# Modulation columns in two passes, Q and K weights in three loads, and a new order of work in an adaLN block (sliding-window attention, then a gMLP mixer)

## The chip, the cores and the metric

One core of one Trainium2 chip runs the kernel. The metric is the device time of one execution in microseconds (us); lower is better. TensorE is called PE, VectorE DVE, ScalarE ACT, GpSimd POOL and SyncE SP, as in the profile.

## The reference, cut to what matters

```python
mod = (silu(c) @ w_mod).reshape(1, 6, 1, 448)      # c: (1, 448), w_mod: (448, 6*448)
sa, ca, ga, sb, cb, gb = mod[:, 0..5]
h = layernorm(x) * (1 + ca) + sa                   # x: (1, 2048, 448), bf16
q, k, v = split(h @ wqkv)                          # 16 heads of 28, wqkv: (448, 3*448)
p = softmax(where(0 <= i - j < 256, q k^T * 28**-0.5, -1e9))
x = x + ga * ((p v) @ wo)
h = layernorm(x) * (1 + cb) + sb
z = gelu(h @ w_in)                                 # w_in: (448, 1792), tanh form
z1, z2 = z[..., :896], layernorm(z[..., 896:])
g = w_sp @ z2 + b_sp                               # w_sp: (2048, 2048), over the sequence
x = x + gb * ((z1 * g) @ w_out)                    # w_out: (896, 448)
```

## The kernel before, in words

The sequence of 2048 rows is cut into 16 tiles of 128 rows, and the tiles into six blocks of 1, 1, 2, 4, 4 and 4 tiles (`blocks` in `PARAMS`). Each engine runs one fixed list of instructions. A small planner holds all operations (`Op`) with their dependencies; a hand-stored list, `ORDER` (L164 to L224), names them by number in the order in which they are put into the engines' lists. Behind a slash stand the choices of buffer (a bank of PSUM, a slot of SBUF), and behind a point the choice of engine where an operation may run on more than one. `Planner.schedule` reads the list, and `Planner.emit` turns every dependency, and every reuse of a buffer, into a semaphore wait. An engine works its own list strictly in order, so a waiting instruction holds all that stand behind it.

**The start.** The row `c` is loaded by ACT's queue (L473), copied in two pieces to a padded row `crz` (`cz0`, `cz1`, L519 and L520; the padding is zeroed by `zc`, L518), turned into columns by four tiny matmuls (`c_cols`) and passed through SiLU into `sc_sb` (L522). Between them PE has 30 matmuls on zeros (`warm0` to `warm29`, L1068 to L1071; the first 12 are 512 wide, the others 256), whose result nobody reads. `mod_cols` (L526 to L540) makes the columns of `sa` and `ca`: eight sums of four matmuls each, `modA0_0` to `modA1_3`, 32 matmuls with a moving operand one column wide; DVE then adds 0 or 1 and writes `modT` (`modAe`, L539). All eight wait for both halves of the modulation weights, `wmodA0` on SP's queue and `wmodA1` on ACT's (`load_dup`, L463 to L467).

The 448 input features do not divide into four chunks of 128, so chunk 1 and chunk 2 overlap: the chunks start at features 0, 128, 192 and 320. `load_dup` loads the overlapping 64 rows twice, in two transfers of 256 rows. `load_ov` (L455 to L461) leaves the doubled rows out: three transfers, one of chunks 0 and 1, one of chunk 3, and one of the upper half of chunk 2.

Each x tile is normalised: statistics on DVE (`l1_*st0`, `ag`, `ve`, L557 to L564), the power -1/2 on POOL (`l1_*rs`, L565), and the scaled tile `xn` on DVE, ACT or POOL (L578, L579, L608). Blocks 0 to 2 are transposed by PE against an identity (`tr`), and the result is multiplied by 1 + `ca` and shifted by `sa` when it is moved from PSUM to `hT` (L641 on ACT, L646 on DVE). Blocks 3 to 5 are transposed by DMA from SP's queue (L663) and modulated in place (`hm`, L655). The raw Q and K weights `wqk_raw` come by two `load_dup` transfers and are copied into the padded form `WQK` by eight copies, `wqkf0_0` to `wqkf1_3` (L679 on DVE, L680 on ACT): one for each chunk 0 to 3 of each half of the heads.

**Attention.** `project` (L719 on) makes Q and K (`qk`, four matmuls for each group of four heads) and V (`v`), moved from PSUM by `qke` (L740 on ACT, L743 on DVE) and `ve` (L751, L754). `S{j}_{u}` are the scores of query tile j, `E{j}_{u}` their exponentials on ACT (L841), `M` the mask on POOL (L847), `PV` the product with V, then come transposes and normalisation (`oq`, `rec`, `nrm`, `oT`), the product with `wo`, and the residual `x1`. One `S` fills PSUM banks for two `E`, and the next `S` in these banks waits for the `E`. `PT` holds the exponentials in 11 slots, which are handed from an `E` to the `PV` that reads it and on to a later `E`.

**The mixer.** After a second normalisation (`l2`, `x2`, `h2T` by DMA, `h2m`), `z2m` and `z1m` are the two halves of `h @ w_in` (`w_in_sb`). Their GELUs run on ACT (`z2g` L945 and L949, `z1g` L968). For five tiles `z2m` is made early and parked raw (`z2e`, L939 on DVE, L942 on ACT). `G` is the product with `w_sp`, whose transposed tiles are read by DMA over SP's queue (L1008) into space freed by attention; `ga`, `gu` (L1037, L1039), `out` and `fin` (L1059) finish the rows, and SP's queue stores them (L1061). Exp and GELU need different function tables on ACT; the switch is an instruction of its own, `ACT_TABLE_LOAD`.

Of the kernel before, what the change touches and what calls it, by code (L numbers as in the profile page):

```python
# [168 lines left out]
148/2 149 155 156 150 151 177/3 176.1/3 178 157.1 486/1 233 98/7 28 99 100 152 101 487 179 123/0 124 125 126 127.1 234 93/1 94 95 96 102.1 97.1 27
103/2 6 104 105 106 107.1 235 238 236 241 18 322 88/0 89 90 91 92 242 243 244/4 138/0 19 139 140 141 245.1/1 142 485/0,0 320 399 108/2 109 110 111  # L170
489/2 158/1 159 160 112 181/3 161 162 180 182 482/2 15 501/1,0 505/4 401 246.1/3 402 198/1 17 199 163/0 164 200 201 165 247.1/2 166 403 202.1 203/3
204 205 206 193/1 194 195 196 502/7 508/1,0 207 218/3 219 167 483 220 188/0 221 248 222.1 189 190 191 192.1 249 197 183/1 184 185 186 213/2 214 187.1
215 216 217.1 509/3 208/3 209 506 511/8 318 210 488/0 323 503 490 491 492/0 493 494.1/1 522/0,1 523/9 211 212.1 526/1 251 228/1 319 223/2 224 225 229
250 230 231 232 316 317 226 227 252 507/0 253 254 321 324 512 510 504 255 529/1,0 530/3 276/3 405 513/0 266/1 267 268 261/2 262 325 326 327/2 331
330.1/3 269 533/10 527 270 277 329/0 263 264 524 536/1,0 539/5 537/0 334 278 279 280.1 271/0 272 311/1 265.1 273 312 514 313 314 274 275.1 550/1,0
296/3 328.1/1 315 297 298 299 300.1 515.1/0 404 406 256/1 257 291/0 258 259 400 407 551/4 552 557/1,2 292 293 294 554/6 260.1 286/1 287 288 289 561/8
564/2,0 516/2 295.1 538/0 558/2 534 540 535 525 528 495/1 408 409 531 532 555 562 332 559 290.1 281/1 282 567/7 578/0,1 283 284 541/0 517/0 518 542
543.1/0 565/3 285.1 579/1 519 520 585/0,2 333 335.1 336.1 544/0 496/1 497 498 499 582/0 917 521 560/0 563 566 568 553 556 337 500 589/10 586/5 569/0
570 592/2,1 593/3 914 545/1 546 547 548 916 412.1/3 369/0 370 371 338.1 583 947 349/3 350 945 549 372 373.1 595/8 606/0,1 607/6 351 610/9 352 364/1
587 365 366 367 353.1 946 613/0,2 915 588/0 614/7 571.1/0 572/1 590 591 596 580 581 584 368.1 594 354/1 355 356 620/0,1 597/0 573/0 574 575 410.1/1  # L180
416 948 949 615 576 617/4 344/2 931/3 577 345 346 347 621/1 623/10 608 357 611 358 413.1/0 960 348.1 962 932 598 950 933 920 634/1,0 934 935 936 414
937 938 618 635/0 306/1 307 411/2 308 309 939 641/1,2 599.1/0 301/0 302 1426 303 304 417 310.1 384/1 638/8 385 386 387 961 600/0 922 645/5 648/0,2 963
964 965 305.1 616/0 619 609 388.1 612 646 622 624 339/1 340 642/3 651/2 662/1,2 639 341 342 636 625/0 637/0 652 649/6 650 643 644 647 640 626 627.1/1
415 418.1 420.1 663/1 669/0,1 343.1 359/1 360 361 362 653/0 374/0 375 376 377 666/7 667 664 673/5 676/1,2 654 670/9 671 679/4 363.1 601/1 602 603
628/2 378.1 629/0 677/3 630 631 951 952.1/1 923 632 633 690/2,0 691/0 421.1 966 604 694/2 605 389/0 390 391 392 697/1,2 394/1 395 396 419.1 967/0
698/10 393.1 442/0 397 919 701/8 398.1 674 443 444 445 704/1,0 655.1/0 379/1 380 446.1 672/0 675 702 975 1428 381 382 953 954/1 955 656/0 383.1 707/6
718/2,0 705/5 665 722/1 699 723 680 678 719/4 668 681/0 657/1 658 682 683.1/0 720 659 660 661 990 991 725/1,0 726/3 727 729/7 730 437/0 438 439 440
452/1 441.1 959.1 976 453 454 455 732/1,2 724/0 721 456.1 728 432/1 433 434 435 977 978 436.1 735/9 746/0,2 684/0 918 969/1 731 733/1 968 695 692 736
# [12 lines left out]
1146 1150 1017.1 888 891 1148 1177 1149 1019 1147 1151 1179 1324 1314/3 1313 1311 1038 1325 1347/0 1348 1180/0 1152/2 1312 1316 1326/5 1315 1181 1349
1335/4 1338/6 1339 1337 1182 898 1331/7 1350 1351 1332 1341 1330 1328 1352 1039 1183 1184 880/0 1040 1433 1129/1 1154 1018.1 899/0 1153 902 1030 892
904 895 896 889 1028 1031 1033 1034 1032 1427 881/2 1451 1131 882 1041 1042/1 1329 905/0 1044/2 1122/1 1123 1106/3 1132/3 1185 1124 1327 906 907.1/1
1371/2 1373 1336 1107 1334 883 1333 884 885 1108 1340 1186 1343 1155 1156 1372 1133 1342 1130 1125 1126 1043 1157 1376/5 1375 1201/1 1202 1374 1045
908/2 1135 1377 1379 1207 1378 1134 1137.1 909/2 910 1204 1203 911 912 1050 1205 1187/0 1380/2 1127 1109 1447 1158 1110 1051 1381 1206 1188 913 1383/0
1385 1384 1074/0 1136.1 1111 1112 1128 1193 1386 1191 1208/2 1215/1 1217 1052 1219 1382 1387 1048.1 1189 1192 1190 1046 1220 1053 1054 1218 1442
1353/3 1049.1 1437 1358/2 1357 1355 1055 1076 1056 1075 1450 1059.1/1 1299/1 1057.1/2 1077 1078 1060 1194/3 1047 1243/0 1248 1245 1058 1356 1209 1210
1211 1212 1079 1354 1216 1388 1080 1249 1359 1361 1196 1305/0 1221 1222/1 1244 1300 1362/2 1457 1213 1214 1448 1364 1441 1360 1195 1197 1247 1246
1250/2 1229/1 1302 1443 1234 1301 1233 1232 1456 1231 1304 1444 1224 1303 1159/0 1163 1160 1435 1306 1223 1252 1165 1062 1064.1 1063 1368/3 1225 1446
1235 1090/0 1162 1061.1 1407/1 1161 1230 1226 1227 1363 1453 1409 1307 1410/0 1412 1164 1366 1365 1408 1251 1253 1198 1228 1236/1 1271/1 1274 1275  # L210
# [73 lines left out]
def bass_adaLN_cond__sliding_block__mixer_gmlp__prompt_kernel(  # L284
# [13 lines left out]
    S, D, H, DH = 2048, 448, 16, 28  # L298
# [139 lines left out]
    def mm(e, out_, lhsT, rhs, st, sp, **kw):  # L438
        return e.matmul(out_, lhsT=lhsT, rhs=rhs, start=st, stop=sp, **kw)  # L439
# [688 lines left out]
```

## Time and profile before

| | us |
|---|---|
| median of 3 runs | 272.41 (272.1 to 272.92) |
| the profiled execution | 271.65 |
| its span, first to last instruction | 269.9 |
| PE busy | 260.3 (96%) |
| DVE busy | 171.8 (64%) |
| ACT busy | 132.0 (49%) |
| POOL busy | 101.2 (37%) |

Busy time counts pipelined matmuls with their modelled ends, so 96% of PE is not 96% of its best rate. The shares are averages over a start of some 17 us, an attention stretch to about 111 us, and a mixer stretch to the end, in which different engines are full.

### The profile page before, as it was taken

Reading aid. Unit: us, or ns where it says so; the run is one execution under the profiler, and the core shown is the slowest. Engines: PE = TensorE matmul, PEld = TensorE weight load, DVE = VectorE, ACT = ScalarE, POOL = GpSimd, SP = SyncE. Lnnn points to the kernel's source line nnn. Section 1 sums busy time; section 2 is a strip of 40 time slices with the busy share of each in tenths; the row PEclk is TensorE's granted clock in tenths of the full one; section 3 lists DMA queues with packets and bytes.
Section 4 is the critical chain, followed back from the end, with each engine's and each line's share of the span. In section 5 each row is a group of like instructions: output and inputs, shape, how many; then the busy total and the mean of one; then the engine's idle time right before and its main releaser. Section 6 shows DMA issues by size and latency. Waiting matters only on the chain.

```text
span 269.9 us, 6339 instructions
## 1 busy us (share of the span) xinstructions
PE 260.3 (96%) x2660; PEld 126.4 (47%) x2689; DVE 171.8 (64%) x413; ACT 132.0 (49%) x177; POOL 101.2 (37%) x160
## 2 busy tenths in 40 slices
PE   7989999999999999999999999999999999999995
PEld 2756445554544454344444444444444444444553
DVE  5789989778889998798986723115242132265444
ACT  5688999999999998986675300000000001000000
POOL 3174789798879996575322300000000000000000
PEclk9999999999999999999999999999999999999999
DMA  7955163691679421637599991000000000000214
GB/s 222 343 188 72 22 163 89 82 163 22 75 122 305 74 52 26 111 73 123 116 220 181 184 192 31 2 0 0 0 2 0 0 0 2 17 0 0 69 53 137
DMA packets 60811, 23.85 MB, mean 88 GB/s; under 512 B 49839, under 2 KB 60654, under 8 KB 60782
## 3 DMA queue, kind: packets, MB, share of 16 engines
q1 hardware_dynamic: 60507, 22.98, 40.9%
q10 hardware_dynamic: 274, 0.46, 0.6%
q8 instruction: 21, 0.34, 0.5%
q14 instruction: 9, 0.07, 0.1%
HBM read 9.53 MB, written 1.84 MB: 42 GB/s over the span
## 4 chain that ended last, share of the span: by engine, by line
PE 79%; DVE 9%; ACT 5%; POOL 3%; issue 2%; DVEq 0%; POOLq 0%
PE ps L439 79%; ACT PT L841 5%; DVE w_out_sb L897 1%; DVE QKT L743 1%; POOL PT L847 1%; POOL hT L655 1%; DVE hT L655 1%; DVE st_all L557 1%; DVE wo_sb L788 1%; DVE oq L873 1%; POOL xn L578 1%; DVE WQK L679 1%; DVE ve_all L564 1%; DVE xn L578 0%; DVE Vaug L754 0%
## 5 line engine op out<-in xcount | busy, mean ns | idle before, releaser
L841 ACT ACTIVATE PT<-ps 128x1024 bf16<-128x1024 f32 x90 | 84.9, 1034 | 3.9 <-PE ps L439 3.5
L1037 DVE TENSOR_TENSOR tmpg<-ps,bsp_bc 128x512 bf16<-128x512 f32 x28 | 18.8, 687 | 58.8 <-PE ps L439 58.6
L968 ACT ACTIVATE z1T<-ps 128x512 bf16<-128x512 f32 x28 | 15.4, 600 | 79.6 <-PE ps L439 79.6
L439 PE MATMUL ps<-QKT,z 128*128 128x512 bf16 x223 | 51.2, 379 | 0.1
L847 POOL TENSOR_SCALAR_AFFINE_SELECT PT<-PT 128x512 f32<-128x512 f32 x60 | 37.5, 647 | 4.0 <-ACT PT L841 3.9
L565 POOL TENSOR_TENSOR rs_all<-ve_all,neghalf 128x1 f32<-128x1 f32 (+2 forms) x30 | 19.9, 666 | 39.1 <-DVE ve_all L564 39.0
L439 PEld LDWEIGHTS ps<-QKT,z 128*128 128x128 bf16 x224 | 21.8, 98 | 26.4 <-ACT z1T L968 0.3
L439 PE MATMUL ps<-hT,WQK 128*128 128x512 bf16 (+2 forms) x179 | 30.9, 304 | 3.0 <-issue 0.8
L439 PE MATMUL ps<-w_in_sb,hT 128*128 128x448 bf16 (+1 forms) x128 | 29.2, 354 | 0.1
L439 PE MATMUL ps<-hT,w_in_sb 128*128 128x512 bf16 (+1 forms) x105 | 27.1, 380 | 0.4 <-DVE hT L655 0.2
L439 PE MATMUL ps<-w_spD,z 128*128 128x512 bf16 x110 | 26.4, 379 | 0.2
L439 PE MATMUL ps<-w_spC,z 128*128 128x512 bf16 x106 | 25.8, 379 | 0.3
L439 PE MATMUL ps<-w_out_sb,z1T 128*128 128x448 bf16 (+2 forms) x119 | 21.5, 342 | 0.0
L557 DVE BATCH_NORM_STATS2 st_all<-z2raw 128x6 f32<-128x448 bf16 x32 | 18.8, 610 | 3.7 <-ACT z2raw L949 2.3
L439 PEld LDWEIGHTS ps<-hT,WQK 128*128 128x128 bf16 x192 | 14.4, 97 | 13.1 <-DVE QKT L743 1.2
L557 DVE BATCH_NORM_STATS2 st_all<-x_sb 128x6 f32<-128x448 bf16 x32 | 19.4, 614 | 1.5 <-DMA x_sb<-in_A_x_dram 1.4
L743 DVE CAST QKT<-ps 128x512 bf16<-128x512 f32 (+2 forms) x34 | 18.5, 558 | 2.6 <-PE ps L439 2.5
L439 PE MATMUL ps<-QKT 28*128 28x128 bf16 x720 | 18.3, 217 | 0.8 <-ACT QKT L740 0.5
L1059 DVE TENSOR_TENSOR fin<-ps,x_sb 128x448 bf16<-128x448 f32 (+2 forms) x17 | 9.8, 595 | 13.6 <-PE ps L439 10.5
L439 PEld LDWEIGHTS ps<-QKT 28*128 28x128 bf16 x720 | 10.4, 92 | 15.3 <-ACT PT L841 10.3
L439 PEld LDWEIGHTS ps<-w_in_sb,hT 128*128 128x128 bf16 (+1 forms) x128 | 10.2, 96 | 15.5 <-issue 5.9
L439 PEld LDWEIGHTS ps<-w_spC,z 128*128 128x128 bf16 x112 | 11.0, 98 | 13.2
(75 smaller groups left out, 304.5 us busy)
## 6 DMA issues: line engine op xcount, KB each, us to landing
wmod_sb<-in_w_mod_dram SPq DMA_DIRECT2D x8, 224.0 KB, 4.6
w_in_sb<-in_B_w_in_dram SPq DMA_DIRECT2D x8, 224.0 KB, 3.2
out_dram<-fin SPq DMA_DIRECT2D x16, 112.0 KB, 1.8
x_sb<-in_A_x_dram SPq DMA_DIRECT2D x3, 448.0 KB, 7.6
wqk_raw<-in_A_wqkv_dram SPq DMA_DIRECT2D x2, 452.0 KB, 6.0
bsp_bc<-in_B_b_sp_dram SPq DMA_DIRECT2D x1, 512.0 KB, 4.2
wmod_sb<-in_w_mod_dram ACTq DMA_DIRECT2D x1, 448.0 KB, 4.1
wmod_sb<-in_w_mod_dram SPq DMA_DIRECT2D x1, 448.0 KB, 4.9
```

Source lines behind the costliest of these rows:

```text
L439: return e.matmul(out_, lhsT=lhsT, rhs=rhs, start=st, stop=sp, **kw)
L557: st = [dve("%sst%d" % (name, i), prio, dve_ns(D), lambda e, i=i, s_=s_: e.bn_stats(st_all[:, slot, t, i, :], s_()), deps, tens) for i, s_ ...
L564: v = dve(name + "ve", prio, 75, lambda e: e.tensor_scalar(ve_all[:, slot, t0:t1], mv_all[:, slot, t0:t1, 1], EPS, None, ALU.add), deps)
L565: r = pool(name + "rs", prio, 420 + 148 * n, lambda e: e.tensor_tensor(rs_all[:, slot, t0:t1], ve_all[:, slot, t0:t1], neghalf[:, t0:t1], ...
L578: return e.tensor_scalar(dst, src, rs_all[:, slot, t:t + 1], nm_all[:, slot, t:t + 1], ALU.mult, ALU.add)
L655: return e.tensor_scalar(hT[:, c_, cols], hT[:, c_, cols], modT[:, base_col + 4 + c_:base_col + 5 + c_], modT[:, base_col + c_:base_col + ...
L743: return e.tensor_copy(QKT[:, g, cols], ps[:, ten.slot, 0:w])
L841: e_op = P.op("E%d_%d" % (j, ui), pr, [("act", 925, lambda e, e_in=e_in, e_out=e_out: e.activation(e_out(), e_in(), ACT.Exp, scale=SCALE)) ...
L847: ready = pool("M%d_%d" % (j, ui), pr - 50, pool_ns(512), lambda e, pt=pt, pat=pat, cm=cm, cmp=cmp: e.affine_select(out=pt32(pt.slot), in_ ...
L968: g = P.op("z1g%d_%d" % (tb, ft), pr - 19, [("act", act_ns(512), lambda e: e.activation(z1T[:, ft, tb * 512:(tb + 1) * 512], ps[:, ten.slo ...
L1037: a = dve("ga%d_%d" % (tb, ft), pr, dve_ns(512), lambda e, tb=tb, ten=ten, tg=tg: e.tensor_tensor(tmpg[:, tg.slot, :], ps[:, ten.slot, :], ...
L1059: fs.append(dve("fin%s%d" % (nm, t), pr, dve_ns(c1 - c0), lambda e, t=t, ten=ten, ft_=ft_, c0=c0, c1=c1: e.tensor_tensor(fin[:, ft_.slot, ...
```

## The change

It does four things.

- `modA` is no longer made by `mod_cols`. There are 16 operations of two matmuls: first chunks 2 and 3 of all eight columns, each waiting only for `wmodA1`, then chunks 0 and 1, waiting for `wmodA0`. The number of matmuls is the same, 32. `mod_cols` is still used for `modB`.
- `wqk` is loaded by `load_ov` (three transfers without the doubled rows) in place of `load_dup` (two).
- A copy `wqkf{g}_{c}` waits only for the transfer that holds its chunk, and a `qk` matmul only for the copy of its chunk; before, both waited for all.
- `ORDER` is new from end to end: positions, engines and buffers of all operations.

```diff
-    t_wqk = load_dup("wqk", -95.5, wqk_raw, A_wqkv, 0, 904, order=t_wmA)
+    t_wqk = load_ov("wqk", -95.5, wqk_raw, A_wqkv, 0, 904)
+    for o in t_wqk:
+        o.order += t_wmA
...
-    t_modA, m1 = mod_cols("modA", -50, (0, 1), 0, t_wmA, CH, 128)
+    mA_ten = Ten(B_D, guard=True)
+    m1 = []
+    for h in (1, 0):
+        for col in range(8):
+            def fn(e, h=h, i=col // 4, mc=col % 4, col=col):
+                last = None
+                for kc in (2 * h, 2 * h + 1):
+                    last = mm(e, ps[:, mA_ten.slot, col:col + 1], wmod_sb[:, kc, i * D + CH[mc]:i * D + CH[mc] + 128], sc_sb[:, kc:kc + 1],
+                              h == 1 and col == 0 and kc == 2, h == 0 and kc == 1, skip_group_check=True)
+                return last
+            m1.append(pe("modA%d_%d%s" % (col // 4, col % 4, "h" if h else ""), -50, 52, fn, [t_wmA[h], t_sc], [mA_ten], order=m1[-1:]))
+    t_modA = [dve("modAe", -49.9, 80, lambda e: e.tensor_tensor(modT[:, 0:8], ps[:, mA_ten.slot, 0:8], zero_one[:, :], ALU.add), m1 + t_zo, [mA_ten])]
...
-                ("pool", 620, lambda e, d=dst, s_=src: e.tensor_copy(d, s_))][0:2 if r0 else 3], t_wqk, port=True))
+                ("pool", 620, lambda e, d=dst, s_=src: e.tensor_copy(d, s_))][0:2 if r0 else 3], [t_wqk[(0, 0, 2, 1)[c_]]], port=True))
...
-                    e, ps[:, ten.slot, 0:n_], stat(k), mov(k), k == 0, k == 3), [deps, hT_op[b][k]], [ten], order=ops[-1:]))
+                    e, ps[:, ten.slot, 0:n_], stat(k), mov(k), k == 0, k == 3), [deps[k] if isinstance(deps, dict) else deps, hT_op[b][k]], [ten], order=ops[-1:]))
...
-                ops, ten = chain("qk%d_%d" % (b, g), p_, t_wqkp[u // 2] + [z_qk],
+                ops, ten = chain("qk%d_%d" % (b, g), p_, {k: [t_wqkp[u // 2][k]] + ([z_qk] if k == 2 else []) for k in range(4)},
```

What the new list makes of the engines' orders, where it differs most:

- PE: before, `warm0, warm1, c_cols, warm2 to warm11, modA0_0, warm12 to warm14, modA0_1 to modA1_3`, then transposes and the other warm matmuls. After: `warm0 to warm15`, the four `tr0`, `warm16, warm17, c_cols, warm18 to warm20, tr1_0_0`, the 16 parts of `modA`, `warm21 to warm27`, and on.
- DVE: `cz0`, `cz1` and `zc` stand behind the statistics of tile 0 and tile 1; before, they stood ahead of them. Four of the eight `wqkf` are on DVE (before: six), one on ACT (two), three on POOL (none).
- ACT: `xn1` stands ahead of the SiLU. Up to the second exponential there are, after `modT`: four `hT` moves, one `wqkf`, nine `qke`, `E0_0`, four `qke`. Between the second exponential and the last `S`, ACT has 3 `ve` (before 5), 4 `qke` of 256 columns (2), 3 of 512 (2), none of 128 (1), and 2 `z2e` (4); the move of the second half of `hT2` is there in both.
- ACT at the end of attention: before, `E15_4, E15_5`, one table load, the GELUs. After: `E15_4`, table load, `z1g0_5, z1g0_4`, table load, `E15_5`, table load, the other GELUs. `E15_5` takes over the `PT` slot of `E14_1`, and so waits for `PV14_1`.
- PE at the end of attention: the six `PV14` stand behind `S15_4` and behind `z2m7`; before, they stood ahead of `S15_4`. Eight 512-wide `z1m` matmuls stood ahead of `S15_4` before, five do after.
- POOL: 13 `xn` (before 9), 24 `h2m` (17), 8 `hm` (7), 11 `x2` (10), 12 `nrm` (14), and the three `wqkf`.
- SP: the three loads of Q and K weights, `x2`, the V weights, the gate weights' first half, two loads of `wo`, `x3`, `x4`, the last load of `wo`, the gate weights' second half. Before, the first `wo` load and the gate weights stood ahead of the V weights.

More of the change, by code (lines that the diff above doesn't have):

```diff
@@ L169 @@
[L169 to L176, printed above, removed]
@@ new lines @@
+495/7 185.1/3 103 104 112/7 113 114 247 250 186/3 187 188.1 115 116 251 97/6 252 16 254.1/1 105 98 253.1/0 106 99 100 101 329 330 325 256.1/2 107/0
+108 327 14 109 110 111 494/0,0 498/1 258 117/0 118 119 120 499 331 167/2 168 169 328 170 171.1 121 190/1 197/0 189 191 412 172/3 173 174 255.1/3 175
+510/0,1 176 198 199 511/0 200 414 491/2 202/3 203 201.1 212/0 213 214 215 207/1 208 257 209 210 514/3 492 496 204 205 415 517/0,1 216 222/0 223 224
+225 226.1 211 206 515 192/3 193 194 260 195 518/5 520/10 227/2 196.1 228 229 230 231 217/1 218 219 220 221.1 500/0 408 497 501/0 531/1,0 532/4 535/2
@@ new lines @@
+457 764 769/2,0 698 717/0 702 709 712 772/6 715 705 770/2 718/0 458 459 757 719 720.1/1 783/1,0 784/8 787/4 992 476/0 477 478 479 980.1 460.1 436/1
+437 1000 788 790/1,2 480.1 765/0 773 1439 768 785 794/3 795 761 771 758 438 774/0 775 791/5 439 440.1 797/0,2 800/10 466/0 721/1 467 468 798/9 469
+749/0 776.1/0 792 481/1 968.1 967.1 965.1 482 483 484 932 811/1,2 815/7 470.1 966.1 471/0 472 812/6 998.1 473 474 485.1 750/1 938 937 751 752 818/2,0
+822/0 753 1001 1002 777/2 475.1 789/0 801 936 786 796 799 939 819/1 982.1 793 816 754 722/1 820 1003 723 930 931 825/1,0 828/10 826/3 724 725 1016
@@ new lines @@
+1009 842 844 845 849 871/5 884/3 1122/1 1128/3 1127 1126 1123 858/0 882/7 879 895/0,1 896/9 859 860/0 861/1 1125 1124 1024 862/0 863 864 1022 865
+1013.1 1130 902/2,0 1129 834/1 835 995.1 1034 1035 1011.1 866 899/4 836 1445 837 1326/2 1331/6 1028.1 1332 1327 1329 903/8 1026 1046 1012.1 906/2
+909/2,0 910/10 1330 1038.1/0 1436 1039 1317/7 1319 838 1010.1 1353/3 1025 1036/2 1328 1037 1182/2 1183 1187 1184 1186 1188 1185 872 1334 1047 869 1354
+1044 1045 876 1333 1359/6 1048 1438 877/0 885 883 897 880 870 873 912/5 1357 1318 1355 1435 1356 886/0 1322/2 907 1321 1358 1154/0 1155 1156 1159 1157
@@ new lines @@
+1251 1459 1267 1303 1269 1273/3 1275 1274 1302 1304 1289 1290 1291 1561/1 1292 1468 1469 1276 1492 1543/2 1562 1305 1306 1307 1503/5 1277 1504 1505
+1278 1279 1526 1293 1470 1473/3 1474 1475 1476 1466 1471/2 1477/1 1493 1494 1478 1527 1448 1528 1472 1544 1545 1546 1547/1 1529/2 1495/0 1506 1461
+1563 1564 1496 1565/0 1566 1507/0 1479/2 1480 1481 1482 1508 1483/0 1530 1531/6 1555/5 1556 1485/1 1486 1487 1488 1484 1489/0 1659/2 1660 1557 1558
+1532 1463 1559/2 1533 1534 1647/0 1497/5 1677/4 1490 1648 1649 1650 1560 1535/2 1536 1548 1498 1405 1537/7 1499 1651/0 1652 1653/1 1538 1539 1540
@@ new lines @@
+1541/3 1500 1501/1 1671/3 1451 1672 1654 1655 1661 1656 1641/7 1678 1679 1549/5 1550 1551 1552 1502 1553/0 1554 1657/0 1673 1674 1680 1513/6 1514
+1675/2 1450 1607/1 1515/0 1665/3 1666 1453 1608 1667 1668 1542 1567/5 1568 1681/1 1579/4 1580 1658 1569/1 1425/1 1427 1669/3 1429/7 1670 1509/0 1510
+1457 1431 1430 1426 1428 1433 1682 1570 1662 1663/3 1642 1643 1511/2 1644 1645/0 1646 1581/3 1517/2 1455 1609 1676 1516 1575/6 1576 1577/0 1610 1611/0
+1601/7 1602 1603 1604 1664 1605/2 1606 1619/4 1620 1621 1622 1582 1623/1 1518 1432 1683/1 1521/4 1687/0 1691/5 1522 1692 1512 1519/3 1595/2 1684
@@ L225 @@
+1693/2 1694 1578 1523/0 1612 1583/6 1685/2 1584 1688 1596 1597 1598 1520 1524 1698/5 1624 1695/4 1689/3 1690 1585 1586 1599/1 1600 1587/1 1699 1589/7
+1590 1696 1686 1697/2 1591 1588 1592 1700 1613/1 1614 1615 1616 1593/2 1594 1625/2 1617/2 1618 1637/3 1626 1627/0 1701 1638 1639/3 1640 1633/5 1628
+1634 1629/6 1630 1571/7 1635/3 1636 1631/2 1632 1572 1573/1 1574
 """
```

89 lines of the change are left out of this document (37 added, 52 removed).

## The prediction

> **What bounds the kernel now.** I read the stretches first (busy time of each engine), then the timelines of PE, DVE and ACT at the start, then ACT and PE at the end of attention. Columns of the first view: from and to, length, busy us and count for PE, weight loads, DVE, ACT, POOL, then granted clock, DMA share, GB/s.
>
> ```profile
> 8.85:16.60 7.75, 6.53 (x100) 5.36 (x99) 7.52 (x29) 6.84 (x19) 2.82 (x5) 1.00 1.05 317
> 16.60:108.68 92.08, 88.84 (x1682) 45.43 (x1697) 80.90 (x181) 88.55 (x103) 75.66 (x110) 1.00 0.51 97
> 108.68:160.00 51.32, 50.93 (x317) 22.13 (x323) 39.98 (x115) 31.58 (x47) 20.29 (x32) 1.00 0.83 148
> ```
>
> 16.60 is the start of the second exponential, `E0_1`; 108.68 that of the last scores, `S15_4`. Between them ACT idles 92.08 - 88.55 = 3.53 us and PE 3.24: both are full, so neither can gain much alone. After 108.68 PE is never seen waiting. The end is thus: the time at which `S15_4` issues, plus the PE work that is left then, plus new PE waits after it.
>
> The start (start us, length, engine, line; in brackets the idle time before and what ended it):
>
> ```profile
> 1.50 1.04 PE L439 MATMUL ps<-warm 128*128 128x512 bf16 x2 [1.50 <-POOL one L497]
> 2.47 0.26 PE L439 MATMUL ps<-one,crz 1*128 1x1 bf16 x4
> 2.67 4.45 PE L439 MATMUL ps<-warm 128*128 128x512 bf16 x10
> 6.91 0.29 PE L439 MATMUL ps<-sc_sb,wmod_sb 128*128 128x1 bf16 x4
> 7.06 0.80 PE L439 MATMUL ps<-warm 128*128 128x256 bf16 x3
> 7.66 0.89 PE L439 MATMUL ps<-sc_sb,wmod_sb 128*128 128x1 bf16 x28
> 9.42 1.04 PE L439 MATMUL ps<-warm 128*128 128x256 bf16 x8
> 11.40 1.63 PE L439 MATMUL ps<-hT,WQK 128*128 128x128 bf16 x26 [0.67 <-DVE WQK L679]
> ```
> ```profile
> 8.85 1.50 ACT L641 ACTIVATE hT<-ps,modT 128x128 bf16<-128x128 f32 x4 [2.07 <-PE ps L439]
> 10.23 0.64 ACT L680 ACTIVATE WQK<-wqk_raw 128x512 bf16<-128x512 bf16 x1
> 12.00 1.34 ACT L740 ACTIVATE QKT<-ps 128x128 bf16<-128x128 f32 x6 [0.27 <-PE ps L439]
> 13.31 1.02 ACT L841 ACTIVATE PT<-ps 128x1024 bf16<-128x1024 f32 x1
> ```
>
> PE spends 1.50 to 8.55 on warm matmuls and `modA`; DVE's `modT` follows at 8.58, the first `hT` at 8.85. PE's pace changes although the clock column says 1.00: ten 512-wide warm matmuls start (4.45 - 0.61)/9 = 0.427 us apart (0.61 is the row of the first alone), three 256-wide at 7.06 some 0.21, eight at 9.42 some 0.11. It doubles between 7.5 and 8.7.
>
> The end of attention on ACT, and the length of a `PV` set on PE:
>
> ```profile
> 109.13 1.94 ACT L841 ACTIVATE PT<-ps 128x1024 bf16<-128x1024 f32 x2 [0.51 <-PE ps L439]
> 111.09 1.28 ACT L968 ACT_TABLE_LOAD   x1
> 112.38 1.09 ACT L968 ACTIVATE z1T<-ps 128x512 bf16<-128x512 f32 x2
> 113.35 1.74 ACT L949 ACTIVATE z2raw<-ps 128x896 bf16<-128x896 f32 x2
> ```
> ```profile
> 117.59 0.89 PE L439 MATMUL ps<-PT,Vaug 128*32 128x128 bf16 x48
> ```
>
> **Part 1, `modA`.** The split lets half of it start when `wmodA1` lands (issued 1.34, 4.1 to land: 5.4) and not when `wmodA0` does (1.71 + 4.9 = 6.6). It gains nothing, because `sc_sb` now comes later than both. POOL clears `warm` first, at 0.78 for 0.52, so PE starts at 1.36. Ahead of `c_cols` stand 12 x 0.427 = 5.12 (to 6.48), four 256-wide at 0.21 (7.32), four transposes at half that (7.75), two 256-wide (8.17); `c_cols` 0.26 to 8.43. A pace that doubles near 8 takes off 0.1. The DVE side is earlier (statistics of tile 0 from 2.87, of tile 1 at 4.3, then `xn0` 0.41, copies of 0.20, `zc` at 6.1), and `xn1` on ACT (0.81) ends at 7.0. SiLU 0.17 from 8.4, `modA` 32 x 0.03 (28 in 0.89) plus 0.16 for the last to end: 9.75; `modT` 0.17. The exp table load (1.28) and `exp0` (0.20), before in ACT's idle time, now follow the SiLU at 8.57 and end at 10.05. First `hT` at 10.0, **1.2 later**. If the pace doubled at 5 us, 3.64/0.427 = 8.5 warm matmuls would be done by then, the rest at half price would bring `c_cols` to 6.8 and `hT` to 8.65. I take the late value, which is the pace of the trace; both ends stay for the range.
>
> **Part 2, loads and copies.** The two loads carry 904 KB, the three 904 x 448/512 = 791: 113 KB less, 0.36 us at 317 GB/s. They landed near 9 us (2.70 + 6.4), while the copies began at 10.23: cost and gain nothing, hidden behind `modT`, even more with `modT` later. One more issue on SP (0.49) delays `x2` (3.76), whose statistics run at 12.18 without waiting for a DMA. The second gate load moves from 6.84 on SP behind the last `wo` load, to about 13.7 (issues of 1.71 and 2.33 ahead of it); with 4.6 to land, 18.3, before a gate matmul at about 19.5 (18.14 before): hidden with 1.2 to spare. Three copies go to POOL, which shows none; between a 512-column clear (0.52) and a 512-column `hT` in place (0.77) I take 0.77, as it reads and writes. From 9.0 they end at 10.5, ahead of the `qk` that need them (11): nothing; at double the price 0.7 late on one chunk.
>
> **Part 3, from `hT` to `E0_1`.** Before 16.60 - 8.85 = 7.75. After, ACT is the longest: four `hT` 1.50, a copy 0.64, nine `qke` at (1.34 - 0.28)/5 = 0.21, 1.92, `E0_0` 1.02, four `qke` 0.85, `S` 0.40: 6.33. With 0.3 for PE's answers 6.6, so `E0_1` starts at 16.6: **the 1.2 lost is won back, 0.0**. POOL's `xn3` ends near 14.9 (statistics of tiles 5 and 6 now precede its `nm`), ahead of need. PE has then done the same matmuls as before.
>
> **Part 4, the attention stretch.** By the rows (0.55 a `ve`, 0.28, 0.41 and 0.63 a `qke` of 128, 256 and 512, 0.55 a `z2e`), ACT has before 5 x 0.55 + 0.28 + 2 x 0.41 + 2 x 0.63 + 4 x 0.55 = 7.3, after 3 x 0.55 + 4 x 0.41 + 3 x 0.63 + 2 x 0.55 = 6.3: 1.0 less. PE's part before `S15_4` loses three 512-wide matmuls (0.22) and `PV14` (0.89): 1.55 less. So `S15_4` can come 1.0 (ACT rules) to 1.55 (PE rules) earlier; I take **-1.3**. POOL gains four `xn` at 0.79, seven `h2m` at 0.57, an `hm` 0.77, an `x2` about 0.8, less two `nrm` at 0.94: +6.9 against 16.4 of idle, counted as nothing; without that cover masks, hence `PV` and exponentials, come late. DVE is lighter.
>
> **Part 5, after `S15_4`.** The PE work moved there: **+1.55**. ACT has two more table loads, 2.56. Clock from `S15_4`: `E15_4` ends 1.40, load 2.68, two GELUs 3.77, load 5.05, `E15_5` 6.02, load 7.30, two `z2g` 9.04 (before 115.09 - 108.68 = 6.41). PE: five matmuls to 1.1, waits for `E15_4` to 1.45, `z2m7` (16 of that kind took 2.92, eight 1.4) to 2.85, one more 3.07, waits for the bank of `z1g0_5` to 3.3, then for that of `z1g0_4` to 3.83, `PV14` to 4.75, waits a little for `oq14`, and reaches `z2m5`, which needs `E15_5`, after it is done. Waits: 0.35 + 0.23 + 0.28 + 0.1, some **+0.7** (PE lost nothing here before). Everything later has its bank back in time.
>
> Sum on the span: 0 - 1.3 + 1.55 + 0.7 = **+0.9**, 270.8; the profiled execution would be 272.6. The median lies 0.76 over the profiled one (272.41 - 271.65), so I put it on the median: **273.3**. A change under 0.3%, 0.8 us, can't be told from none here.
>
> **The rivals.** *Early pace.* PE's pace doubles earlier, so that the queue ahead of `c_cols` is short: `hT` at 8.65, `E0_1` 1.35 earlier (8.65 + 6.6 = 15.25), 0.9 - 1.35 = -0.45: 272.0. For it: nothing in the kernel sets the moment; against: the trace has it late. The Trainium skill ("TensorE: Matmul & The Clock Gate", Part 1) says that the array runs at half rate until it was busy for one full window of about 3.4 us, and that the window runs free of the kernel. That would put the doubling 3.4 to 6.8 us after the first matmul, by chance; the trace, 6.0 to 7.2 after 1.50, agrees with the late end only.
>
> *Table loads stop PE (slower).* The 2.6 us by which ACT falls behind at the end of attention reach PE in full, not 0.7: +1.9, 275.2. It decides where the bank that PE wants is one whose GELU is among the delayed; my walk leaves only 0.05 to 0.4 us there, from `z2m4` to `PV15`. Against: ACT idled 0.48, 0.51, 0.16 and 1.05 from 116 to 124, so it can catch up.
>
> *Fewer waits in attention (faster).* The new order also fills half of the 3.53 us that ACT idled: 0.9 - 1.8 = -0.9, 271.5; with an early pace as well 270.2. For it: `qke` spread otherwise; against: POOL is fuller, and both engines were 96% full.
>
> *It doesn't do what it says.* Neither the two passes nor the waits per chunk have anything to save when `modT` comes last; then only the order counts. That is in the forecast.
>
> **How the numbers follow.** Forecast 0.42, its own range 272.3 to 274.3 (0.5 each way for parts 4 and 5, 0.5 for part 3); early pace 0.24; table loads 0.17; fewer waits 0.17. Slower by over 0.3% (above 273.2): half of the forecast 0.23, table loads 0.16, early pace 0.03: 0.42. Faster (below 271.6): early pace 0.08, fewer waits 0.14, rest 0.03: 0.25. Within: 0.33. Range 270.2 (early pace and fewer waits) to 275.5 (table loads and a late copy).
>
> **What would show it.** `c_cols` after 7.5, the first `hT` near 10, `E0_1` near 16.6; ACT's two extra table loads around 109 to 113 with PE waits of under 1 us beside them; `S15_4` near 107.4. Wrong if `c_cols` runs before 7, if PE shows more than 2 us of waits after `S15_4`, or if `S15_4` is off by more than a microsecond.

## The result, and the profile after

| | before | after |
|---|---|---|
| median of 4 runs each, on one chip | 272.25 us (272.03 to 272.92) | 274.85 us (274.5 to 279.52) |
| ratio, 95% interval | | 1.0087 (1.0062 to 1.0111) |
| the profiled execution, its span | 271.65, 269.9 | 274.9, 273.1 |
| a later series: 17 runs before, 6 after | 271.87 (271.22 to 273.36) | 276.92 (275.06 to 278.07), ratio 1.019 (1.016 to 1.0221) |

The change is slower. The first ratio leaves the run at 279.52 out. Its runs lie in steps, which follow the clock that TensorE was granted on the mean over a run: 274.5 to 274.9 at 0.999 to 1.00, 279.52 at 0.988. The reason is one of the findings; times below are given with that clock where it matters. The two profiled executions both have 1.00.

The stretches view of the kernel after, cut at its first `hT` (10.00), at `E0_1` (16.58) and at `S15_4` (109.70); columns as before (length; busy us and count of PE, weight loads, DVE, ACT, POOL; granted clock, DMA share, GB/s):

```profile
10.00:16.58 6.58, 5.48 (x85) 4.17 (x86) 6.41 (x22) 5.46 (x20) 4.52 (x7) 1.00 1.06 303
16.58:109.70 93.12, 87.77 (x1632) 44.52 (x1646) 79.57 (x176) 87.23 (x101) 78.71 (x116) 1.00 0.44 96
109.70:160.00 50.30, 49.64 (x356) 21.86 (x361) 38.99 (x109) 33.97 (x48) 22.33 (x37) 1.00 0.91 160
```

In the middle line PE is idle 93.12 - 87.77 = 5.35 us; before it was 92.08 - 88.84 = 3.24. PE's total work is the same (260.3 before, 260.2 after), so the whole loss is PE's idle time. Worked out from such stretches (length less busy), in us, with the kernel of the first experiment beside it:

| PE idle | before | after | after, w_in loads early |
|---|---|---|---|
| 0 to 16.6 | 2.72 | 3.06 | 2.59 |
| 16.6 to 91 | 2.90 | 2.51 | 2.52 |
| 91 to `S15_4` (at 108.68, 109.70, 108.08) | 0.34 | 2.84 | 1.25 |
| `S15_4` to the last matmul | 0.81 | 1.30 | 1.29 |
| after the last matmul | 2.84 | 3.14 | 3.14 |

Of 3.2 us, 2.5 lie between 91 and `S15_4`. The timeline of PE there, after:

```profile
90.17 0.93 PE L439 MATMUL ps<-wmod_sb,sc_sb 128*128 128x448 bf16 x4
92.55 1.70 PE L439 MATMUL ps<-w_in_sb,hT 128*128 128x448 bf16 x8 [1.46 <-DVE w_out_sb L910]
94.18 0.40 PE L439 MATMUL ps<-QKT 28*128 28x128 bf16 x16
```

`z2m0`, the first product with `w_in`, starts 1.46 late, the next scores stand behind it, and ACT, whose exponentials wait for them, idles 1.93. The name in the bracket misleads: `z2m0` does not depend on the products that write `w_out_sb`. It waits for its `h2m` (the last ended at 87.75), for a bank (free at 90.86) and for all eight loads of `w_in_sb`. Those stand on SP's queue like this:

```profile
78.40 1.11 SPq L788 DMA_DIRECT2D w_in_sb<-in_B_w_in_dram  x1
79.56 1.19 SPq L923 DMA_TRANSPOSE hT<-xn  x1
80.79 1.30 SPq L1021 DMA_TRANSPOSE QKT<-in_B_w_sp_dram  x1
82.13 1.13 SPq L788 DMA_DIRECT2D w_in_sb<-in_B_w_in_dram  x1
83.31 0.98 SPq L792 DMA_DIRECT2D w_out_sb<-in_B_w_out_dram  x2
84.33 0.48 SPq L788 DMA_DIRECT2D w_in_sb<-in_B_w_in_dram  x1
84.85 0.47 SPq L792 DMA_DIRECT2D w_out_sb<-in_B_w_out_dram  x1
85.36 1.69 SPq L788 DMA_DIRECT2D w_in_sb<-in_B_w_in_dram  x3
```

Asked for the last of the three alone (the view of a source line; durations in ns, then from issue to landing in us), the profile says:

```profile
L788 SPq DMA_DIRECT2D w_in_sb<-in_B_w_in_dram x1: 644/644/644, 86.4 to 86.4; - x1
DMA to landing us min/median/max: 5.7/5.7/5.7
```

It landed at 92.1, and `z2m0` ran 0.45 later. In the kernel before, the last three `w_in` loads and `z2m0` read:

```profile
82.24 1.73 SPq L775 DMA_DIRECT2D w_in_sb<-in_B_w_in_dram  x3
90.94 1.77 PE L439 MATMUL ps<-w_in_sb,hT 128*128 128x448 bf16 x8
```

The last of them was issued at 83.50 and landed at 88.65, ahead of need. In the new list five of the eight loads stand behind `h2T5` and `h2T4`, which wait for normalised tiles, where before all eight stood ahead of `h2T4`; the loads wait for nothing themselves. The part of the chapter on the change that tells of SP's queue ends before these loads and does not name them.

The start after, on PE and on DVE:

```profile
1.37 5.31 PE L439 MATMUL ps<-warm 128*128 128x512 bf16 x16 [1.37 <-POOL warm L498]
7.05 0.25 PE L439 MATMUL ps<-one,crz 1*128 1x1 bf16 x4
7.68 0.94 PE L439 MATMUL ps<-sc_sb,wmod_sb 128*128 128x1 bf16 x32
10.02 0.29 PE L439 MATMUL ps<-ident,xn 128*128 128x128 bf16 x2 [0.61 <-DVE modT L555]
10.83 0.23 PE L439 MATMUL ps<-hT,WQK 128*128 128x128 bf16 x1 [0.42 <-ACT hT L654]
```
```profile
8.95 0.29 DVE L692 COPY WQK<-wqk_raw 64x512 bf16<-64x512 bf16 x1 [0.35 <-DMA wqk_raw<-in_A_wqkv_dram]
9.27 0.17 DVE L577 TENSOR_SCALAR ve_all<-mv_all 128x2 f32<-128x2 f32 x1
9.47 0.29 DVE L692 COPY WQK<-wqk_raw 64x512 bf16<-64x512 bf16 x1
9.79 0.17 DVE L555 TENSOR_TENSOR modT<-ps,zero_one 128x8 f32<-128x8 f32 x1
```

`modA` ended at 8.62, but `modT` came 1.2 later: on DVE it stands behind a copy that waits for a transfer of Q and K weights. And the end of attention on ACT, where the two extra table loads are seen (the second and third):

```profile
110.15 1.02 ACT L854 ACTIVATE PT<-ps 128x1024 bf16<-128x1024 f32 x1 [0.52 <-PE ps L439]
111.19 1.28 ACT L981 ACT_TABLE_LOAD   x1
112.49 1.08 ACT L981 ACTIVATE z1T<-ps 128x512 bf16<-128x512 f32 x2
113.59 1.28 ACT L854 ACT_TABLE_LOAD   x1
114.89 1.02 ACT L854 ACTIVATE PT<-ps 128x1024 bf16<-128x1024 f32 x1
115.93 1.28 ACT L962 ACT_TABLE_LOAD   x1
```

### The profile page after: what moved, and what is told of

Its sections match the earlier page's. It is cut to its first block, busy times and chain, and to the rows that moved or that the text cites. A ratio compares the mean times of both kernels' runs of the same rounds, so it can differ in the third digit from the quotient of the medians.

```text
span 273.1 us, 6347 instructions
## 1 busy us (share of the span) xinstructions
PE 260.2 (95%) x2660; PEld 126.3 (46%) x2689; DVE 170.9 (63%) x402; ACT 131.7 (48%) x176; POOL 109.3 (40%) x174
## 4 chain that ended last, share of the span: by engine, by line
PE 81%; ACT 9%; DVE 4%; DMA 2%; issue 1%; SPq 1%
PE ps L439 81%; ACT PT L854 8%; DMA wqk_raw<-in_A_wqkv_dram 2%; DVE z L952 1%; DVE hT L659 1%; DVE oq L886 1%; DVE WQK L692 1%; DVE ve_all L577 0%; SPq L470 0%; ACT L981 0%; DVE w_out_sb L910 0%; ACT z1T L981 0%; DVE fin L1072 0%; DVE x_sb L905 0%; DVE st_all L570 0%
## 5 line engine op out<-in xcount | busy, mean ns | idle before, releaser
L439 PE MATMUL ps<-QKT,z 128*128 128x512 bf16 x220 | 49.3, 379 | 0.2
L439 PE MATMUL ps<-w_spD,z 128*128 128x512 bf16 x110 | 25.5, 379 | 0.1
L439 PE MATMUL ps<-w_out_sb,z1T 128*128 128x448 bf16 (+2 forms) x119 | 23.2, 341 | 0.0
L668 POOL TENSOR_SCALAR hT<-hT,modT 128x256 bf16<-128x256 bf16 (+1 forms) x32 | 19.9, 632 | 4.2 <-DMA hT<-xn 4.0
L591 POOL TENSOR_SCALAR xn<-x_sb,rs_all,nm_all 128x512 bf16<-128x512 bf16 x24 | 18.8, 789 | 6.9 <-DVE nm_all L582 3.5
L756 DVE CAST QKT<-ps 128x512 bf16<-128x512 f32 (+2 forms) x28 | 16.6, 597 | 2.9 <-PE ps L439 2.8
```

Of the source, the lines that this page charges most:

```text
L591: return e.tensor_scalar(dst, src, rs_all[:, slot, t:t + 1], nm_all[:, slot, t:t + 1], ALU.mult, ALU.add)
L668: return e.tensor_scalar(hT[:, c_, cols], hT[:, c_, cols], modT[:, base_col + 4 + c_:base_col + 5 + c_], modT[:, base_col + c_:base_col + ...
L756: return e.tensor_copy(QKT[:, g, cols], ps[:, ten.slot, 0:w])
```

## The experiments

Edits are shown as changes of an engine's list of operations. Ratios are to the kernel before on the same chip, with 95% intervals.

**The late load (`a_win`), and modT first (`a_modt`).**

```diff
 SP:  wmod5_1
+     win3_1 win0_1 win1_0 win2_0
      h2T2 h2T3 wmod5_0 win2_1 h2T5 win3_0 h2T4 wsp0_5 win1_1 wout2 wout0
-     win3_1
      wout4
-     win0_1 win1_0 win2_0
      wsp0_7
```

> The changed kernel, with four loads of w_in (win3_1, win0_1, win1_0, win2_0) moved on SP's queue from behind h2T4 to right behind wmod5_1, where the queue is idle for 7.5 us. Theory A (the last w_in load, landed at 92.10, is what z2m0 waits for at 91.06 to 92.55): the wait goes, z2m0 starts near 91.1, when the sum of tile 10 (ended at 90.86) frees its bank; S13_2 and everything up to S15_4 comes 1.4 earlier (S15_4 near 108.3), and the time is 1.4 lower, some 273.4. Rival (the w_out multiplications on DVE, which the profile names as the releaser): z2m0 still starts near 92.5 and the time stays at 274.8. Third way (it is given back before the end, since ACT or POOL is the bound there): z2m0 starts early, but the time falls by under 0.5.

273.24 to 275.37, median 274.28, ratio 1.0083 (1.0059 to 1.0106); the three runs at clock 1.00 took 273.24, 273.25 and 274.04. Its profile, at 1.00 with a span of 271.5:

```profile
90.08 0.93 PE L439 MATMUL ps<-wmod_sb,sc_sb 128*128 128x448 bf16 x4
90.84 1.70 PE L439 MATMUL ps<-w_in_sb,hT 128*128 128x448 bf16 x8
```

The wait is gone, `S15_4` comes at 108.08, and the span is 1.6 shorter: theory A. The DVE products named by the bracket were not moved. The other three runs, at 0.994, took 274.5 to 275.4; what they waited for no profile shows. Because of them the ratio is hardly below the change's first (1.0087), and the change itself did not run beside this kernel: the gain rests on the runs at full clock (273.2 to 274.0, the change 274.5 to 274.9) and on the profiles.

```diff
 DVE: l1_3ag
+     modAe
      wqkf0_2 l1_2ve wqkf1_2
-     modAe
      wqkf1_3
```

> The changed kernel, with DVE's modAe (which writes modT) moved ahead of wqkf0_2, l1_2ve and wqkf1_2. The last sum of modA ends at 8.62, so modT comes near 8.8 and the first hT near 8.95, 1.05 earlier. If the start passes through to the end: E0_1 at 15.5 (16.58 now), time 1.0 lower, 273.8. Rival (the last transfer of Q and K weights, landed at 9.9, and its four copies, which end at 11.25, come next): the qk matmuls wait for the copies, E0_1 moves by 0.3 or less and so does the time.

275.93 to 280.87, median 278.15, ratio 1.0212 (1.0178 to 1.0246). The late load is still there (it landed at 95.3, PE waited 2.71 for it) and clock was lost, so the time says little; the start says more:

```profile
9.30 0.17 DVE L555 TENSOR_TENSOR modT<-ps,zero_one 128x8 f32<-128x8 f32 x1 [0.33 <-PE ps L439]
9.50 0.29 DVE L692 COPY WQK<-wqk_raw 64x512 bf16<-64x512 bf16 x1
10.02 1.52 DVE L692 COPY WQK<-wqk_raw 64x512 bf16<-64x512 bf16 x3
```
```profile
11.60 0.23 PE L439 MATMUL ps<-hT,WQK 128*128 128x128 bf16 x1 [1.55 <-DVE WQK L692]
```

`modT` is 0.5 earlier (`modA` ended later in this run), and the first `qk` 0.8 later than in the change: it waits for the copies. The rival's mechanism holds, the copies come next; its size does not, as PE's wait of 1.55 was followed by half clock from 13.35, and `E0_1` came at 18.69.

**E15_5 ahead of the table loads (`a_e15`), and all three edits (`a_three`).**

```diff
 ACT: E15_4
+     E15_5
      z1g0_5 z1g0_4
-     E15_5
 PE:  S15_4
+     PV14_2 PV14_5 PV14_4 PV14_3 PV14_0 PV14_1
      z1m0_4_b3 z1m0_2_a0 z1m0_2_a1
-     z1m1_4_a0
      z1m0_4_a1 (z2m7)
+     z1m1_4_a0
      z1m1_4_a3 z1m1_4_r
-     PV14_2 PV14_5 PV14_4 PV14_3 PV14_0 PV14_1
-bank of z1m0_4_a 6, of z1m1_4_a 7, of z1m0_2_b 6
+bank of z1m0_4_a 7, of z1m1_4_a 6, of z1m0_2_b 7
```

> The changed kernel with the end of attention of the kernel before: E15_5 right behind E15_4, so that ACT has one table load there and not three; for that the six PV14 stand right behind S15_4, and the banks of z1m0_4, z1m1_4 and z1m0_2 are those of the kernel before. If the two extra loads cost what PE is seen to wait between 109.7 and 125 (0.4 to 0.5): time 0.4 lower, 274.4. If they stop PE in full (2.6 us of ACT): 1.9 lower, 272.9. If the waits come from elsewhere: no change.

277.42 to 280.98, median 280.12, ratio 1.0266 (1.0231 to 1.03): every expectation missed. In its profile PE waited 2.87 for the late load and 2.15 ahead of `z1m0_4`, and a window at half clock came with each.

> All three edits (early w_in loads, modT first, E15_5 first). If each cost stands on the path and they add up: 1.4 + 1.0 + 0.4 = 2.8 lower, 272.0, as fast as the kernel before. If the start's gain is taken back by the Q and K copies: 273.0. If PE is bound by work alone in between, under 1 lower.

275.41 to 278.47, median 277.58, ratio 1.019 (1.0155 to 1.0225); 275.41 and 275.53 at clock 1.00, that is 2.2 above `a_win`. Its profile shows that the edit had brought waits of its own:

```profile
106.17 0.93 PE L439 MATMUL ps<-wo_sb,oT 128*128 128x448 bf16 x4
108.73 1.24 PE L439 MATMUL ps<-hT,w_in_sb 128*128 128x512 bf16 x5 [1.63 <-DVE x_sb L905]
110.93 0.88 PE L439 MATMUL ps<-PT,Vaug 128*32 128x128 bf16 x48 [0.63 <-POOL PT L860]
```

Bank 7 belongs to `wo12` until `x1_12` has read it, so `z1m0_4` in bank 7 waits 1.63; the `PV14`, now early, wait 0.63 for a mask. So this undoing of the table loads was not clean, and what they alone cost is not told by it.

**The change once more (`after_again`), its code in the old order (`a_oldorder`), a late load in the kernel before (`b_late`), two more table loads (`a_win_loads`).** `a_oldorder` takes all lists from the kernel before; in place of `modA0_0` to `modA1_3` stand the first passes and then the second ones, in place of `wqk1, wqk0` stand `wqk3, wqk2, wqk01`.

> The changed kernel itself, once more, beside the others on one chip. If the granted clock belongs to the program's waits (a PE wait of 1.5 us can cost a window of 3.41 us at half clock, which is 1.7 us), its runs fall into steps: about 274.7 at a mean clock of 1.00, about 276.5 at 0.994, about 278 to 279.5 at 0.988. If they are all at 274.5 to 275, the one run at 279.52 was an accident.

275.06 and 276.08 at clock 0.998, and 276.84, 276.99, 278.03 and 278.07 at 0.992 to 0.994: steps, though not at the values expected. PE's timeline, and stretches of the profiled run (276.84), whose third figure from the right is the clock:

```profile
93.11 1.99 PE L439 MATMUL ps<-w_in_sb,hT 128*128 128x448 bf16 x8 [2.19 <-DVE mv_all L573]
```
```profile
92.00:94.00 2.00, 0.89 (x5) 0.32 (x5) 1.00 (x4) 0.17 (x1) 1.73 (x3) 1.00 0.32 68
94.00:96.00 2.00, 2.00 (x23) 0.76 (x22) 0.82 (x4) 0.84 (x2) 0.06 (x1) 0.59 0.00 0
96.00:98.00 2.00, 2.00 (x8) 0.47 (x6) 2.00 (x3) 1.64 (x2) 2.00 (x4) 0.55 0.02 5
98.00:100.00 2.00, 2.00 (x69) 1.25 (x68) 1.17 (x3) 1.43 (x2) 2.00 (x4) 1.00 0.33 68
```

The same load landed at 92.66 here, the wait was 2.19, and right behind it PE ran at half clock for 3.41 us, which is another 1.7.

> The changed kernel's code (modA in two passes, Q and K weights in three loads, waits per chunk) with the engines' lists of the kernel before. If these parts gain nothing (the prediction): within 0.4 of the kernel before, 271.6 to 272.4. If they gain (here c_cols is early, and the first pass can start when wmodA1 lands at 5.4, not at 6.6): modT 0.4 earlier, near 8.2, the first copies earlier too, and the time some 0.4 lower, 271.5. If three loads in place of two cost: 0.3 higher.

271.43 to 272.63, median 272.23, ratio 1.0006 (0.9991 to 1.0022), clock 0.999 to 1.00 in all 12 runs. In the old order the three parts of the change gain and cost nothing that can be measured; the order makes the difference.

```diff
 SP:  win0_1 win3_0
-     win2_1
      wout4 h2T4
+     win2_1
      h2T7
```

> The kernel before, with one load, win2_1, moved on SP's queue from ahead of wout4 (issued at 83.50, landed at 88.65) to behind h2T4 (issued at 88.37). It would land near 94; z2m0, which starts at 90.94 now, would wait until about 94.4. If a late w_in load is what the new order pays for, the time rises by that wait, 3.3, to some 275.3 in the runs whose clock stays at 1.00, and by 1.7 or 3.4 more where the wait costs a window or two at half clock. If something else in the new order costs the time: under 1 higher, 272 to 273.

273.64 to 278.22, median 275.23, ratio 1.0123 (1.0099 to 1.0147); 273.64 and 275.08 at clock 1.00, less than the 275.3 expected there.

```profile
89.62 0.93 PE L439 MATMUL ps<-wmod_sb,sc_sb 128*128 128x448 bf16 x4
93.68 2.83 PE L439 MATMUL ps<-w_in_sb,hT 128*128 128x448 bf16 x8 [3.13 <-POOL PT L847]
```

One load moved behind a transpose does to the old order what the new order does to itself; in the profiled run, at 0.994, the clock was lost as well.

```diff
 ACT: E15_4 z1g0_5
+     (Exp of a constant)
      z1g0_4 E15_5
```

> The changed kernel with the early w_in loads, and a tiny exponential of a constant between z1g0_5 and z1g0_4: two more table loads on ACT, 1.28 each, and the instruction 0.2, so 2.8 us more on ACT ahead of E15_5. If table loads at the end of attention are nearly hidden (0.4 of 2.6 us reach PE in the change): 0.4 to 1.0 above the kernel with the early loads alone (273.2 at clock 1.00), 273.6 to 274.2. If ACT is the bound there: 2.8 above it, 276.0.

277.77 to 278.65, median 278.21, ratio 1.024 (1.0223 to 1.0258), none of the four runs above clock 0.994; the lowest is the 276.0 of the second theory and one lost window, 1.7.

```profile
111.21 0.75 PE L439 MATMUL ps<-hT,w_in_sb 128*128 128x512 bf16 x3
115.09 0.89 PE L439 MATMUL ps<-PT,Vaug 128*32 128x128 bf16 x48 [3.13 <-ACT z1T L981]
```

At this place the 2.8 us reach PE in full: its wait ahead of `PV14` goes from 0.19 in `a_win` to 3.13, since the bank of `PV14` is the one whose GELU is held up. The change's own extra loads stand behind that GELU, so this prices the place ahead of it, not theirs.

**The code before in the new order (`b_neworder_win`).** Lists of `a_win`; `modA` in one pass where the second pass stood, `wqk1, wqk0` for the three loads.

> The other way round: the code of the kernel before (modA waits for both halves of the weights, Q and K weights in two loads, every copy and qk waits for all) with the engines' lists of the changed kernel and the early w_in loads. If waits per chunk and two passes gain nothing in the new order either: as the changed kernel with the early loads, 273.2 in a run whose clock stays at 1.00. If they carry it (there the copies of chunks 2 and 3 run from 8.29 on, ahead of modT and of the last transfer at 9.9): the copies on DVE start at 9.9, modT stands behind them, E0_1 comes 0.5 to 1.0 later, and so does the end, 273.7 to 274.2.

274.74 to 275.54, median 275.18, ratio 1.012 (1.01 to 1.014), all six runs at clock 0.994. DVE's timeline:

```profile
9.71 0.29 DVE L679 COPY WQK<-wqk_raw 64x512 bf16<-64x512 bf16 x1 [1.03 <-DMA wqk_raw<-in_A_wqkv_dram]
10.03 0.46 DVE L564 TENSOR_SCALAR ve_all<-mv_all 128x2 f32<-128x2 f32 x1
10.52 0.69 DVE L679 COPY WQK<-wqk_raw 64x512 bf16<-64x512 bf16 x1
11.24 0.17 DVE L539 TENSOR_TENSOR modT<-ps,zero_one 128x8 f32<-128x8 f32 x1
```

Here the copy ahead of `modT` waits for the last transfer, `modT` comes at 11.24 and not near 9.8, PE idles 1.61, and a window at half clock follows (from 13.41): `E0_1` at 19.18, not 16.52. So in the new order the waits per chunk, with the three loads, keep `modT` from waiting for the last transfer, and they were worth nothing in the old one. This run undoes the two passes as well, and its ratio and that of `a_win` (1.0083, 1.0059 to 1.0106) just overlap: what the waits per chunk are worth in time is read from the profiles, not shown by the medians.

**Three tries at a better start, with the old lists: `best`, `b_start`, `best2`.**

```diff
 PE:  warm2 to warm8
+     (first passes of modA) warm9 (second passes) tr0_2 tr0_1 tr1_0 tr1_1 tr0_0 warm10 ...
 DVE: xn0
-     l1_3st0 modAe l1_2st0 l1_2ag l1_3ag hT1_0 hT0_0 wqkf0_3 wqkf0_2 wqkf0_0 ...
+     modAe hT1_0 hT0_0 l1_3st0 wqkf0_0 wqkf0_3 wqkf0_2 l1_2st0 l1_2ag l1_3ag l1_2ve ...
```

> The changed kernel's code with the lists of the kernel before, and a start that uses the parts: on PE the first pass of modA right behind warm8, the second behind warm9, five transposes next and the other warm matmuls behind them; the load of chunks 0 and 1 first of the three; on DVE modT and its two hT ahead of the statistics of tile 3, then the copies of chunks 0, 3 and 2. Theory (a start that is earlier reaches the end: E0_1 was 0.55 earlier in the profile with the late load, and every exponential to the 73rd with it): modT near 7.4, first qk near 9.7, E0_1 near 15.5, 1.1 ahead of 16.6, time 270.8 to 271.2. Rival (another resource takes over at once: the last transfer at 9.8, or PE's cold pace without the warm matmuls): E0_1 at 16.3 or later, time 271.6 to 272.

272.34 to 273.59, median 272.59, ratio 1.0033 (1.002 to 1.0046); four of 12 runs at 0.993 to 0.994. PE's timeline of the profiled run, which lost clock from 8.05:

```profile
6.76 0.55 PE L439 MATMUL ps<-sc_sb,wmod_sb 128*128 128x1 bf16 x16 [0.41 <-DMA wmod_sb<-in_w_mod_dram]
8.64 3.51 PE L439 MATMUL ps<-warm 128*128 128x512 bf16 x17 [0.22 <-issue]
```

The first copy is ready at 9.6, but 17 warm matmuls, most of them at half clock, run to 12.15, and the first `qk` starts at 12.26. The rival came true for `E0_1` (17.39 in this run); the time is above what either theory gave.

> The code of the kernel before with the same new start, so modA in one pass waits for wmodA0 (landed at 6.6) behind warm9, and all copies wait for both loads (9.6). If the parts of the change are what makes the early start possible: modT near 7.8, copies from 9.65 on, first qk near 10.6, E0_1 near 16.1, time 271.4, half way. If only the order counts: as the kernel with the parts.

272.43 to 273.67, median 273.31, ratio 1.0053 (1.0035 to 1.0072). `E0_1` at 16.67 in its profile, not near the 16.1 of the first theory. Neither version gains, and as the two intervals overlap, whether the parts matter in this start is not told.

`best2`: both passes behind `warm11`, 22 warm matmuls, `tr0_3` behind `warm14`, `l1_2nm` and `xn2` ahead of `l1_7st0`.

> The changed kernel's code with the lists of the kernel before and a start that takes away what the last two were seen to wait for: PE stays on warm matmuls up to warm11 (no wait for wmodA0, so the clock has no reason to fall), then both passes of modA and five transposes; 22 warm matmuls in place of 30, so that they do not run past the first qk; tr0_3 earlier; the load of chunks 0 and 1 first; on DVE modT and its hT first, then copies, and nm and xn of tile 2 ahead of the statistics of tile 7. If modT, the warm matmuls and the tile 2 chain were the three waits: modT near 8.3, first qk near 10.1, E0_1 near 15.9, time 271.0 to 271.3 against 271.7 before. If the start is held by yet another chain (the second half's copies, ACT's moves): E0_1 at 16.4 or later and no change, 271.6 to 272.2.

271.32 to 272.94, median 271.99, ratio 1.0002 (0.9988 to 1.0015), clock 0.999 to 1.00 in all 12 runs. The start is earlier in the profile (first `qk` 9.65, `E0_1` 16.19, 0.4 ahead), but the lead is gone at the fifth exponential (22.57 against 22.29), behind this line of PE:

```profile
21.57 0.61 PE L439 MATMUL ps<-hT,WQK 128*128 128x256 bf16 x4 [0.85 <-DVE QKT L756]
```

Before, that wait was 0.17; on DVE the move to `QKT` stands behind the statistics of later tiles. Nor is the lead of 0.4 the edit's for sure: `b_late`, whose start is that of the kernel before, had `E0_1` at 16.05 in its profile. What differs there is the moment at which PE's pace doubled: by the clock records of the traces 7.78 before, 5.13 in `b_late` and 5.91 in `best2`. No version tried beats the kernel before.

## Why the prediction was right or wrong

The forecast was 273.3 in 270.2 to 275.5, slower the likeliest; the median of 274.85 lies inside, 1.6 above the forecast. Its sum on the span was +0.9; it is +3.2. That the median still lies inside is luck: the top of the range was set for table loads that stop PE in full and a late copy, not for a late load. By the prediction's own signs it was wrong: `S15_4` was to come near 107.4 and came at 109.70, off by 2.3.

- **Part 1.** The first `hT` at 10.0 is right to the hundredth, for a wrong reason. PE's pace doubled near 5.6, `c_cols` ran at 7.05 and not at 8.43, `modA` ended at 8.62 and not at 9.75: the early pace came, without the early `hT` that the rival took from it. What brought `hT` back to 10.0 is DVE's queue, where `modT` stands behind a copy that could start only at 8.95, when its transfer had landed. The moment of the doubling is not the kernel's: in the 13 traces that record it, full clock begins 3.1 (`best`) to 6.4 us (`a_oldorder`) after the first matmul, and the 6.3 of the one profile before was a late draw. That the split gains nothing held in the old order (1.0006).
- **Part 2.** "Hidden behind `modT`" was wrong in the new order: a copy stands ahead of `modT`. The waits per chunk let it run at 8.95; where all copies wait for the last transfer it ran at 9.71 (`b_neworder_win`). A copy on POOL takes 0.61 to 0.68 in the profile after, the price taken was 0.77.
- **Part 3.** `E0_1` at 16.58, forecast 16.6.
- **Part 4, the step that failed:** "`S15_4` can come 1.0 (ACT rules) to 1.55 (PE rules) earlier; I take -1.3". It came 1.02 later. The work in the stretch did fall (by the middle lines of the two views, ACT's by 1.3 and PE's by 1.1), but the step put new waits at nothing: it was read from the full engines alone, and SP's queue was not walked, where the `w_in` loads now stand behind the transposes. The late load explains 1.6 (`a_win`: 108.08), and `b_late` shows that such a load alone costs 1.8 and 3.2 in its two runs at full clock. The remaining 0.7 are other waits: with the load early, `S15_4` is 0.6 earlier and not 1.3, and PE idles 1.25 from 91 on where it idled 0.34. What sets these was not tried.
- **Part 5.** +1.55 of work and +0.7 of waits were forecast, 2.25. From `S15_4` to the last matmul PE has 1.34 more work and 0.49 more idle time, and the end behind the last matmul is 0.30 longer: 2.13. The rival that table loads stop PE in full is refuted for this change by the 0.5, though how much of it is theirs stays open; `a_win_loads` bears out its condition, that the bank which PE wants decides.
- **It doesn't do what it says.** As put there: with the old lists the parts are worth nothing, so only the order counts. In the new order the profile of `b_neworder_win` speaks against it.
- **What the sum left out:** a lost window of clock. The range held the first median; that of the later series, 276.92, lies above it.

Open: the span of `a_win` at full clock (271.5) is still 1.5 above that of the kernel before (269.9; 1.53 before rounding). The idle table places 0.9 of it between 91 and `S15_4`, 0.5 behind it and 0.3 at the end, less 0.5 gained ahead of 91; PE's busy time is 0.35 longer. Which choices of the list make these was not tried.

## What to carry to other kernels

Walk the DMA queue as closely as the busy engines: a load that waits for nothing can still be late if it stands behind a transfer that waits, and moving it cost nothing that these runs show. Don't trust the releaser that a profile names for a wait on several semaphores; list what the instruction depends on and look up when each was done. A part that gains nothing in one order can shorten a wait in another, so test parts in both.

## What the runs showed of the hardware

**A wait of PE can be paid twice.** In seven profiled runs the granted clock fell to 0.5 ahead of the kernel's end, for 3.41 us or twice that, and in all but one place a PE wait of 1.5 us or more lies in the 3.41 us ahead: waits of 2.19, 3.13, 2.87 and 2.71 at `z2m0` (clock lost from 94.38, 93.88, 93.96 and 95.27), 2.15 ahead of `z1m0_4` (from 114.44), 3.13 ahead of `PV14` (from 116.26), 1.61 and 1.55 at the start (from 13.41 and 13.35). The exception is `best`, where matmuls of one column and waits of 0.26 and 0.41 came before 8.05. A wait of 1.46 in the profile after cost no clock, and neither did one of 1.63 in that of `a_three`; none of 24 runs of `a_oldorder` and `best2`, whose profiles have no such waits, fell below 0.999. So the length of a wait alone does not decide. Cut each trace into stretches of 3.41 us, counted from the moment at which its full clock begins: all losses but that of `best` follow a stretch in which PE was idle for 1.68 us or more in all, the largest idle time that cost nothing is 1.52 (`a_three`), and the wait of 1.63 lies across an end of a stretch, at 108.47. This is worked out from the traces kept, not tested; in `best` the stretch ahead of the loss has 0.87. The Trainium skill ("TensorE: Matmul & The Clock Gate", "Why this matters for your kernels") advises no idle gaps of PE over about 3 us, as a window of idle time brings half the rate back. The lengths of 3.41 agree with its window (Part 1 of that page); the limit does not: here 1.55 us was followed by half clock, and the measurement decides.

**A landing is not a constant.** The last `w_in` load landed 5.7 us after its issue in one run of the change and 5.9 in another; `a_e15`, with the same queue up to there, had 6.7. An order without room at that place pays a different price each time.

**A copy can be slow beside another engine's.** DVE's 512-column copies of `WQK` took 0.28 to 0.29 each before. Beside POOL's copies of the same kind one took 0.70 in the profile after, two took 0.70 and 0.59 in `a_modt`, and two 0.69 and 0.50 in `b_neworder_win`; the cause was not tested.
